# H3 convolution and linear attention on one core: the shift convolution of four chunks in two parts by time points, 11 of 16 on VectorE and 5 on POOL, and constants in ScalarE's instructions

## The chip, the core and the metric

One core of one Trainium2 chip runs the whole kernel in one launch. The metric is device microseconds from start to end of the program, the median of several runs. The core has five engines that work beside each other, each down a queue of its own: PE (TensorE, matrix products from SBUF into the eight banks of PSUM), DVE (VectorE) and POOL (GpSimd) for element-wise work, ACT (ScalarE) for element-wise functions, and SP (SyncE), which here only issues transfers. An instruction starts when those ahead of it on its engine are done and when the data it reads, and the place it writes to, have been given free by the others.

## The reference, cut

Two blocks that don't depend on each other, over S = 2048 time points and D = 576 channels; their results stand side by side in the output.

```python
def A(q, k, v, shift_k, ssm_k, ssm_D):                  # H3
    k_pad = pad(k, 3 zeros ahead in time)
    k_shift = sum over t of k_pad[:, t:t+S, :] * shift_k[:, 3-t]   # four taps for each channel
    kv = k_shift * v
    y = irfft(rfft(kv, 2S) * rfft(ssm_k, 2S))[:S]        # long convolution, as long as the sequence
    y = y + kv * ssm_D
    return q * y

def B(x, wqkv, wo):                                      # linear attention, 32 heads of 18
    q, k, v = x @ wqkv
    phi = lambda t: where(t > 0, t + 1, exp(t)) + 1e-6
    pq, pk = phi(q), phi(k)
    kv, z = sum over s of pk[s] v[s]^T, sum over s of pk[s]
    return ((pq @ kv) / (pq @ z + 1e-6)) @ wo

out = concat([A(...), B(...)], axis=-1)
```

## The kernel before, in words

**Layout.** Block A is cut into five chunks of channels (`ACH`: four of 128, one of 64). q, k and v lie in SBUF with 128 blocks of time on the partitions, and in each partition 16 time points by the channels. A chunk's k or v is thus 128 x 16 x 128, 2048 elements in a partition (1024 for the last chunk). k comes in two groups (`GRP`: 256 channels, chunks 0 and 1, then 320), which use one buffer in turn.

**The shift convolution** is the unit `cv.chunk.stage.engines`, function `conv`. Stage 0 multiplies k by tap 0 into `a_`. Stages 1 to 3 multiply the shifted k by their tap into `t_` and add `t_` to `a_`. Stage 3 then writes v = `a_` * v over v. That makes eight operations for a chunk, all `tensor_tensor` with both inputs in SBUF. Each letter of the code names the engine of one operation, D for VectorE and P for POOL. `a_` and `t_` are the two halves of the tile `at`, of which there is one buffer. In the profile the multiplications of stage 0 are L492, those of the other stages L494, the additions L495, and the product with v L498.

**The long convolution** is a transform in two steps for the filter h (codes with h) and for v (codes with u). `u1`/`h1` (function `s1`, L537) multiplies one time point at a time, `v[:, b, :]`, by the matrix G: eight matmuls for half of the time points. The result goes from PSUM to the tile `Cu` or `Ch`; `ut`/`ht` transposes it by a transfer; `u2`/`h2` (L560) is the second step, into `SU` or `T`. `pX`, `pT`, `pS`, `pA` (function `prod`: X L572, T L574, S and A L577) form the product of the two spectra, on VectorE or POOL, from SBUF to SBUF. `i1` (L594) and `i2` (L607, L608) go back, and `i2` ends with the product with q on VectorE (L609).

**Block B.** `k.r` (L456) and `q.g.half`, `qt` (L465, L473) project x, of which four transposed groups xT come in turn, two in SBUF at a time; the last step for a group is a memset of one row on POOL (L354). Each projection ends with `phi`: ScalarE takes the exponential from PSUM (L448), then VectorE takes min and max of that and the PSUM bank (L449). Only then is the bank free. `G` (L662) multiplies x by pk; it ends with a copy of one column on VectorE (L652), then a copy on ScalarE (L653). `hc` are constants for the heads, made on POOL (L85 to L102).

**Order.** Nothing is left to a scheduler. The list `ORDER` is written by hand, and its units are recorded one after the other; each engine then runs its own instructions in that order. The digits behind a slash in a unit are places: each names which PSUM slot (0 to 3, two banks each) or which tile of a ring the unit takes. TensorE's unit that takes a slot waits until the engine that last read it is done.

A projection's end, with the bank free behind the second line:

```python
nc.scalar.activation(out=out_ap, in_=ps_ap, func=ACT.Exp, bias=K.neg1[0:n, :])
nc.vector.scalar_tensor_tensor(out=out_ap, in0=out_ap, scalar=1.0, in1=ps_ap, op0=ALU.min, op1=ALU.max)
```

Of the kernel before, what the change touches and what calls it, by code (L numbers as in the profile page):

```python
# [31 lines left out]
ORDER = """  # L32
io ls ix.0.0/0 sin.1.0 wu.1.A/0 wu.2.B/1 dl ix.1.0/1 sin.0.0 hl.0/0 dc/2 hd.0 Wj.A/301 ix.0.1 id xl.2 iw ix.1.1 sin.0.1
hl.1/1 hT.0.D/22 xd.2.DA/030 hd.1 h1.0.0.0.A/11 h1.0.1.0.D/2 hT.1.D/00 wm iv sin.1.1 xl.0 h1.0.0.1.A/3 xd.0.DA/112
h1.0.1.1.A/0 wk lw.1 sw W lw.2 k.11/3 hl.2/1 hd.2 lw.0 k.9/2 k.2/0 k.1/1 k.10/3 kl.0 h1.1.1.1.A/02 k.8/0 cv.0.0.D es
cv.0.1.DD hc h1.1.1.0.A/1 h1.1.0.1.A/3 q.2.1/2 xl.3 q.0.1/0 k.0/1 h1.1.0.0.A/3 ht.0.0/0 qt.0/2 ht.0.1/1 h2.0.1.1.A/00
cv.0.2.PD vl.0/0 cv.0.3.DDD h2.0.1.0.A/3 eps ql.0/1 q.2.0/1 hl.3/2 xd.3.AA/020 q.0.0/3 k.3/2 ht.1.1/1 u1.0.1.1.A/10
k.15/1 u1.0.1.0.A/3 hT.2.D/00 u1.0.0.1.A/2 u1.0.0.0.A/1 cv.1.0.P cv.1.1.DD k.13/3 cv.1.2.DD h2.1.1.1.A/10 h2.1.1.0.A/2
q.3.1/1 h2.0.0.1.A/20 xd.1.T/1 h2.0.0.0.A/3 cv.1.3.DDP q.3.0/2 ut.0.0/1 u2.0.0.0.A/00 q.1.0/3 k.7/1 k.6/0 FT.0.T
u2.0.0.1.A/2 ut.0.1/0 pX.0.0.D/0 qt.1/3 u2.0.1.0.A/11 u2.0.1.1.D/0 k.12/2 u1.1.1.0.A/11 kl.1 k.5/3 u1.1.0.1.A/0  # L40
pX.0.1.D/1 k.14/1 ht.1.0/1 xl.1 u1.1.0.0.A/2 u1.1.1.1.A/3 cv.2.0.D hl.4/1 pT.0.1.D k.4/0 h1.2.1.0.A/02 pS.0.1.D ut.1.1/0
h1.2.1.1.A/1 cv.2.1.DD pT.0.0.P hd.3 pS.0.0.D q.1.1/3 h2.1.0.0.A/32 h2.1.0.1.A/0 G.1/1 cv.2.2.DP h1.2.0.0.A/2 pA.0.1.N
h1.2.0.1.A/0 u2.1.1.1.D/03 zs/01 ut.1.0/1 u2.1.1.0.A/2 pA.0.0.N i1.0.0.0.D/13 i1.0.0.1.A/0 i1.0.1.0.A/1 zz/2
i1.0.1.1.A/3 pX.1.1.D/0 pA.1.1.N vl.1/0 cv.2.3.DDD ht.2.0/0 pT.1.1.D u2.1.0.1.A/10 u2.1.0.0.A/2 ht.2.1/1 FT.1.T
hT.3.a/02 hd.4 G.3/1 cv.3.0.D cv.3.1.DD u1.2.0.0.A/03 lwv pS.1.1.D u1.2.1.1.A/0 G.0/2 cv.3.2.DD u1.2.1.0.A/1 pX.1.0.D/1
pA.1.0.N u1.2.0.1.A/3 G.4/0 h2.2.1.1.A/22 cv.3.3.DDD h2.2.1.0.A/1 ut.2.0/1 G.2/3 h2.2.0.0.D/00 wom lwo i2.0.1/2
h2.2.0.1.A/1 u2.2.0.0.A/03 i2.0.0/0 h1.3.0.1.D/11 ut.2.1/0 h1.3.0.0.A/2 h1.3.1.0.A/3 kv/0 u2.2.0.1.A/2 h1.3.1.1.A/1
pT.1.0.D pS.1.0.D i1.1.1.1.A/03 hT.4.p/01 i1.1.1.0.A/0 cv.4.0.D den/2 cv.4.1.PP ht.3.1/1 u2.2.1.1.D/11 i1.1.0.1.D/3
i1.1.0.0.A/0 pX.2.0.D/0 u2.2.1.0.A/1 M.2.A/2 i2.1.0/3 i2.1.1/0 M.3.A/1 ht.3.0/0 h2.3.1.1.A/12 bc.2/31 st.0 u1.3.1.1.A/00
# [176 lines left out]
def _sine(tc, cpool, K, ri, h):  # L226
    b = slice(8 * h, 8 * h + 8)
    if ri not in K.G:
        K.G[ri] = cpool.tile([128, 16, 128], BF, name="G%d" % ri)
# [1 line left out]
    tc.nc.scalar.activation(out=K.G[ri][:, b], in_=src, func=ACT.Sin, scale=TWO_PI / 8192, bias=K.negpi[:])  # L231
# [22 lines left out]
def kernel(  # L254
# [190 lines left out]

    def phi(ps_ap, out_ap, n):

        nc.scalar.activation(out=out_ap, in_=ps_ap, func=ACT.Exp, bias=K.neg1[0:n, :])  # L448
        nc.vector.scalar_tensor_tensor(out=out_ap, in0=out_ap, scalar=1.0, in1=ps_ap, op0=ALU.min, op1=ALU.max)  # L449

    def b_k(r):
        ps = psum.tile([128, 1024], FP32, name="k_ps")
        rr = r % 4
# [4 lines left out]
        phi(ps[:, 0:D], pk[:, r, 0:D], 128)

    def b_q(g, half):  # L460
        ps = psum.tile([128, 2, 512], FP32, name="q_ps")
        for j in range(2):
            c = 2 * half + j
            for t in range(5):
                nc.tensor.matmul(ps[:, j, :], lhsT=wqk[:, t, 128 * c:128 * c + 128], rhs=xT[g][:, t, :],  # L465
                                 start=(t == 0), stop=(t == 4))
        phi(ps[:], pqT[:, 2 * half:2 * half + 2, g * 512:(g + 1) * 512], 128)

    def b_qt(p):
        ps = psum.tile([128, 512], FP32, name="qt_ps")  # L470
        for t in range(5):
            for i, g in enumerate(PAIR[p]):
                nc.tensor.matmul(ps[64 * i:64 * i + 64, :], lhsT=wqk[:, t, 512:576], rhs=xT[g][:, t, :],  # L473
                                 start=(t == 0), stop=(t == 4))
        phi(ps[:], pq4[:, p, :], 128)


    def conv(ci, stage, eng='DDD'):
# [12 lines left out]
        if stage == 0:
            on[0].tensor_tensor(out=a_, in0=kk[:, 3:19], in1=wb(0), op=ALU.mult)  # L492
        else:
            on[0].tensor_tensor(out=t_, in0=kk[:, 3 - stage:19 - stage], in1=wb(stage), op=ALU.mult)  # L494
            on[1].tensor_tensor(out=a_, in0=a_, in1=t_, op=ALU.add)  # L495
# [399 lines left out]
```

## Time and profile before

| | |
|---|---|
| runs | 157.4, 157.73 and 157.91 us, median 157.73 |
| profiled execution | its span is 156.1 us; the runs' times take in about 1.6 us around the span |
| PE | 148.3 us busy, 95% of the span |
| DVE | 134.2 us, 86% |
| ACT | 130.8 us, 84% |
| POOL | 60.3 us, 39% |
| granted TensorE clock | full in every slice |

Busy time is work done, not work that sets the end: an engine can be busy with something that has time. The stage of the convolutions lies between 23 us, when k has landed, and 100 us. The chain of work that ended last has 62% of its time on PE, 12% on transfers, 11% on ScalarE, 8% on VectorE and 1% on POOL. Rows of a timeline give start, length, engine, line and instruction, the output behind the arrow's head and inputs behind its tail; grouped rows give count, then busy time and the mean in ns.

### The profile page before, as it was taken

Reading aid. Unit: us, or ns where it says so; the run is one execution under the profiler, and the core shown is the slowest. Engines: PE = TensorE matmul, PEld = TensorE weight load, DVE = VectorE, ACT = ScalarE, POOL = GpSimd, SP = SyncE. Lnnn points to the kernel's source line nnn. Section 1 sums busy time; section 2 is a strip of 40 time slices with the busy share of each in tenths; the row PEclk is TensorE's granted clock in tenths of the full one; section 3 lists DMA queues with packets and bytes.
Section 4 is the critical chain, followed back from the end, with each engine's and each line's share of the span. In section 5 each row is a group of like instructions: output and inputs, shape, how many; then the busy total and the mean of one; then the engine's idle time right before and its main releaser. Section 6 shows DMA issues by size and latency. Waiting matters only on the chain.

```text
span 156.1 us, 4608 instructions
## 1 busy us (share of the span) xinstructions
PE 148.3 (95%) x1986; PEld 90.6 (58%) x1986; DVE 134.2 (86%) x169; ACT 130.8 (84%) x162; POOL 60.3 (39%) x70
## 2 busy tenths in 40 slices
PE   7999999999999999999999999999988999999990
PEld 2686564466633456457566558767555656568650
DVE  6989769899899798997899999899999979997530
ACT  4999999989998899959999767997998978897431
POOL 6038701908310974007300019457999050230000
PEclk9999999999999999999999999999999999999999
DMA  2997999999999699999999879977779997636086
GB/s 92 380 294 188 296 300 145 252 296 281 201 178 234 135 312 235 166 231 302 178 171 199 220 134 232 144 139 136 231 156 179 149 325 187 156 117 182 0 231 197
DMA packets 74315, 31.92 MB, mean 204 GB/s; under 512 B 52090, under 2 KB 73653, under 8 KB 74294
## 3 DMA queue, kind: packets, MB, share of 16 engines
q1 hardware_dynamic: 74294, 31.62, 90.7%
q8 instruction: 15, 0.25, 0.6%
q14 instruction: 6, 0.05, 0.1%
HBM read 14.97 MB, written 4.72 MB: 126 GB/s over the span
## 4 chain that ended last, share of the span: by engine, by line
PE 62%; DMA 12%; ACT 11%; DVE 8%; issue 2%; POOLq 2%; POOL 1%; SPq 1%; DVEq 0%; ACTq 0%
PE k_ps L456 10%; PE g_ps L662 10%; PE s_ps L537 8%; PE q_ps L465 6%; DMA q<-in_A_q_dram 6%; PE i_ps L594 5%; PE s_ps L560 4%; PE o_ps L783 4%; DMA Cth<-Ch 3%; DMA Ctu<-Cu 3%; DVE q L609 2%; DVE pqT L753 2%; PE i_ps L607 2%; PE i_ps L608 2%; ACT G L231 2%
## 5 line engine op out<-in xcount | busy, mean ns | idle before, releaser
L456 PE MATMUL k_ps<-wqk,xT 128*128 128x512 bf16 (+1 forms) x160 | 21.5, 286 | 0.0
L537 PEld LDWEIGHTS <-G 128*128 128x128 bf16 x320 | 17.2, 98 | 3.1 <-issue 2.3
L465 PE MATMUL q_ps<-xT,wqk 128*128 128x512 bf16 x80 | 18.4, 380 | 0.0
L309 ACT ACTIVATE Cu<-s_ps 128x1024 bf16<-128x1024 f32 (+1 forms) x19 | 17.3, 957 | 0.4 <-PE s_ps L537 0.2
L456 PEld LDWEIGHTS <-xT 128*128 128x128 bf16 x160 | 11.4, 98 | 10.5 <-issue 0.3
L662 PE MATMUL g_ps<-pk,x_sb 128*128 128x512 bf16 (+1 forms) x128 | 16.5, 286 | 0.0
L309 ACT ACTIVATE V<-i_ps 128x1024 bf16<-128x1024 f32 x16 | 15.5, 1025 | 1.1 <-PE i_ps L594 0.8
L309 ACT ACTIVATE Ch<-s_ps 128x1024 bf16<-128x1024 f32 (+1 forms) x17 | 15.7, 952 | 0.3 <-PE s_ps L537 0.3
L309 ACT ACTIVATE T<-s_ps 128x1024 bf16<-128x1024 f32 x15 | 14.8, 1026 | 0.8 <-PE s_ps L560 0.7
L309 ACT ACTIVATE ob<-o_ps 128x576 bf16<-128x576 f32 (+1 forms) x14 | 8.8, 635 | 7.4 <-PE o_ps L775 4.2
L783 PE MATMUL o_ps<-wo_M,pqT 128*128 128x512 bf16 (+1 forms) x112 | 15.0, 287 | 0.0
L495 DVE TENSOR_TENSOR at<-at 128x2048 bf16<-128x2048 bf16 (+1 forms) x12 | 14.2, 1181 | 0.9 <-POOL at L494 0.4
L449 DVE SCALAR_TENSOR_TENSOR pk<-pk,k_ps 128x576 bf16<-128x576 bf16 x16 | 11.9, 752 | 3.4 <-ACT pk L448 3.2
L309 ACT ACTIVATE SU<-s_ps 128x1024 bf16<-128x1024 f32 x14 | 14.1, 1027 | 0.7 <-PE s_ps L560 0.6
L494 DVE TENSOR_TENSOR at<-k,Wj 128x2048 bf16<-128x2048 bf16 (+1 forms) x12 | 14.1, 1171 | 0.0
L495 POOL TENSOR_TENSOR at<-at 128x1024 bf16<-128x1024 bf16 (+1 forms) x3 | 8.3, 2772 | 14.0 <-DVE at L494 10.9
L609 DVE TENSOR_TENSOR q<-i_ps,q 128x1024 bf16<-128x1024 f32 (+1 forms) x10 | 11.0, 1114 | 3.1 <-PE i_ps L608 2.8
L662 PEld LDWEIGHTS <-x_sb 128*128 128x128 bf16 x128 | 8.4, 97 | 8.9 <-issue 1.2
L448 ACT ACTIVATE pk<-k_ps,neg 128x576 bf16<-128x576 f32 x16 | 11.6, 741 | 1.5 <-PE k_ps L456 1.0
L465 PEld LDWEIGHTS <-wqk 128*128 128x128 bf16 x80 | 7.4, 98 | 9.2 <-issue 1.5
L783 PEld LDWEIGHTS <-pqT 128*128 128x128 bf16 x112 | 7.5, 98 | 7.9 <-issue 1.2
L594 PE MATMUL i_ps<-W,T 64*128 64x128 bf16 x160 | 11.2, 217 | 0.6 <-DVE pqT L753 0.5
(163 smaller groups left out, 336.0 us busy)
## 6 DMA issues: line engine op xcount, KB each, us to landing
x_sb<-in_B_x_dram SPq DMA_DIRECT2D x4, 576.0 KB, 6.9
h_sb<-in_A_ssm_k_dram SPq DMA_DIRECT2D x4, 512.0 KB, 5.8
out_dram<-ob SPq DMA_DIRECT2D x7, 288.0 KB, 4.0
k<-in_A_k_dram SPq DMA_DIRECT2D x1, 1280.0 KB
v<-in_A_v_dram SPq DMA_DIRECT2D x1, 1280.0 KB
q<-in_A_q_dram SPq DMA_DIRECT2D x1, 1280.0 KB, 8.6
wqk<-in_B_wqkv_dram SPq DMA_DIRECT2D x2, 576.0 KB, 8.4
k<-in_A_k_dram SPq DMA_DIRECT2D x1, 1024.0 KB, 8.8
```

The source lines that it names most:

```text
L309: nc.scalar.activation(out=out, in_=in_, func=ACT.Copy)
L448: nc.scalar.activation(out=out_ap, in_=ps_ap, func=ACT.Exp, bias=K.neg1[0:n, :])
L449: nc.vector.scalar_tensor_tensor(out=out_ap, in0=out_ap, scalar=1.0, in1=ps_ap, op0=ALU.min, op1=ALU.max)
L456: nc.tensor.matmul(ps[:, n0:n1], lhsT=xT[r // 4][:, t, rr * 128:(rr + 1) * 128], rhs=wqk[:, t, D + n0:D + n1], start=(t == 0), stop=(t == 4))
L465: nc.tensor.matmul(ps[:, j, :], lhsT=wqk[:, t, 128 * c:128 * c + 128], rhs=xT[g][:, t, :], start=(t == 0), stop=(t == 4))
L494: on[0].tensor_tensor(out=t_, in0=kk[:, 3 - stage:19 - stage], in1=wb(stage), op=ALU.mult)
L495: on[1].tensor_tensor(out=a_, in0=a_, in1=t_, op=ALU.add)
L537: nc.tensor.matmul(ps[:, bi, 0:dc], lhsT=K.G[ri][:, b, :], rhs=xf(b), start=True, stop=True)
L594: nc.tensor.matmul(ps[:, r, g, :], lhsT=s[key, hf][64 * r:64 * r + 64, z, x, 128 * g:128 * g + 128], rhs=K.W[64 * r:64 * r + 64, m, :], st ...
L609: nc.vector.tensor_tensor(out=qs, in0=ps[:, :, 0:dc], in1=qs, op=ALU.mult)
L662: nc.tensor.matmul(ps[:, n0:n1], lhsT=x_sb[:, r, f0:f0 + fn], rhs=pk[:, r, n0:n1], start=(r == 0), stop=(r == 15))
L783: nc.tensor.matmul(pss[i][:, n0:n1], lhsT=pqT[:, c, r * 128:(r + 1) * 128], rhs=B['M'][:, c, n0:n1], start=(c == 0 and not first), stop=(c ...
```

## The change

Two things. Every operation of the convolution of chunks 0 to 3 (engine code `S`) is split over the 16 time points: points 0 to 10, 1408 elements in a partition, on VectorE, and points 11 to 15, 640 elements, on POOL. Chunk 4 keeps its codes. And two constants, -pi in the sines and -1 in the exponential of phi, are given in the ScalarE instruction and no longer as a tile of one column. No unit changes its place in `ORDER`; in the profile after, all operations of the convolution have one line, L487, and the lines behind it are three higher.

```diff
-cv.0.0.D ... cv.0.1.DD ... cv.0.2.PD ... cv.0.3.DDD          (the same codes in ORDER for chunks 1 to 3)
+cv.0.0.S ... cv.0.1.SS ... cv.0.2.SS ... cv.0.3.SSS
...
-    tc.nc.scalar.activation(out=K.G[ri][:, b], in_=src, func=ACT.Sin, scale=TWO_PI / 8192, bias=K.negpi[:])
+    tc.nc.scalar.activation(out=K.G[ri][:, b], in_=src, func=ACT.Sin, scale=TWO_PI / 8192, bias=-math.pi)
...
-    nc.scalar.activation(out=K.sm[:, 1536:1984], in_=K.wi, func=ACT.Sin, scale=TWO_PI / 16, bias=K.negpi[:])
+    nc.scalar.activation(out=K.sm[:, 1536:1984], in_=K.wi, func=ACT.Sin, scale=TWO_PI / 16, bias=-math.pi)
...
-        nc.scalar.activation(out=out_ap, in_=ps_ap, func=ACT.Exp, bias=K.neg1[0:n, :])
+        nc.scalar.activation(out=out_ap, in_=ps_ap, func=ACT.Exp, bias=-1.0)
...
-        on = [nc.gpsimd if e == 'P' else nc.vector for e in eng]
+        def on(n, o, i0, i1, op):
+            for p, b0, b1 in ((0, 0, 11), (1, 11, 16)) if eng[n] == 'S' else ((eng[n] == 'P', 0, 16),):
+                (nc.gpsimd if p else nc.vector).tensor_tensor(out=o[:, b0:b1], in0=i0[:, b0:b1], in1=i1[:, b0:b1], op=op)
...
-            on[0].tensor_tensor(out=a_, in0=kk[:, 3:19], in1=wb(0), op=ALU.mult)
+            on(0, a_, kk[:, 3:19], wb(0), ALU.mult)
...
-            on[0].tensor_tensor(out=t_, in0=kk[:, 3 - stage:19 - stage], in1=wb(stage), op=ALU.mult)
-            on[1].tensor_tensor(out=a_, in0=a_, in1=t_, op=ALU.add)
+            on(0, t_, kk[:, 3 - stage:19 - stage], wb(stage), ALU.mult)
+            on(1, a_, a_, t_, ALU.add)
...
-            on[2].tensor_tensor(out=u, in0=a_, in1=u, op=ALU.mult)
+            on(2, u, a_, u, ALU.mult)
```

VectorE's queue at chunk 0, a piece of the difference (rows with `at` are the convolution, `pk`, `pqT` and `pq` phi; two rows of one form that follow each other are told as x2):

```order
 L449 SCALAR_TENSOR_TENSOR pk<-pk,k_ps 128x576 x6
-L492 TENSOR_TENSOR at<-k,Wj 128x2048
-L494 TENSOR_TENSOR at<-k,Wj 128x2048
-L495 TENSOR_TENSOR at<-at 128x2048
+L487 TENSOR_TENSOR at<-k,Wj 128x1408 x2
+L487 TENSOR_TENSOR at<-at 128x1408
 L449 SCALAR_TENSOR_TENSOR pqT<-pqT,q_ps 128x2x512 x2
 L449 SCALAR_TENSOR_TENSOR pk<-pk,k_ps 128x576
 L449 SCALAR_TENSOR_TENSOR pq_77<-pq_77,qt_ps 128x512
-L495 TENSOR_TENSOR at<-at 128x2048
```

The convolution's places among VectorE's phi operations stay, with 1408 elements in place of 2048.

POOL's queue at chunk 0, a piece of the difference that begins with the last of the head constants and ends with the memset of an xT:

```order
 L101 MEMSET onesr 128x32
 L102 MEMSET onesr 128x8
-L494 TENSOR_TENSOR at<-k,Wj 128x2048
+L487 TENSOR_TENSOR at<-k,Wj 128x640
+L487 TENSOR_TENSOR at<-at 128x640
+L487 TENSOR_TENSOR at<-k,Wj 128x640
+L487 TENSOR_TENSOR at<-at 128x640
+L487 TENSOR_TENSOR v<-at,v 128x5x128
 L396 MEMSET pk 128x16
 L354 MEMSET xT 1x512
```

POOL had one whole operation of chunk 0 here and now has five parts, the last of which writes v; three more parts stand ahead of the head constants (before L85, where POOL had no convolution). The memset of xT comes behind all eight.

POOL's queue at chunk 2 before, from the memset of the second k buffer on (T is the product of chunk 0's spectra, `hp` the filter of chunk 4):

```order
L408 MEMSET k 1x960
L574 TENSOR_TENSOR T<-SU,T 128x2048
L495 TENSOR_TENSOR at<-at 128x2048
L644 MEMSET wo_M 128x576
L523 COPY hp<-h_sb 64x2048
```

And after:

```order
L408 MEMSET k 1x960
L487 TENSOR_TENSOR at<-k,Wj 128x640 x2
L487 TENSOR_TENSOR at<-at 128x640
L577 TENSOR_TENSOR T<-SU,T 128x2048
L487 TENSOR_TENSOR at<-k,Wj 128x640
L487 TENSOR_TENSOR at<-at 128x640
```

T was the first work behind the memset and now comes behind three parts of chunk 2's convolution, which wait for the second k.

More of the change, by code (lines that the diff above doesn't have):

```diff
@@ L34 @@
 hl.1/1 hT.0.D/22 xd.2.DA/030 hd.1 h1.0.0.0.A/11 h1.0.1.0.D/2 hT.1.D/00 wm iv sin.1.1 xl.0 h1.0.0.1.A/3 xd.0.DA/112
[L35 to L38, printed above, removed]
@@ L39 @@
-q.3.1/1 h2.0.0.1.A/20 xd.1.T/1 h2.0.0.0.A/3 cv.1.3.DDP q.3.0/2 ut.0.0/1 u2.0.0.0.A/00 q.1.0/3 k.7/1 k.6/0 FT.0.T
+h1.0.1.1.A/0 wk lw.1 sw W lw.2 k.11/3 hl.2/1 hd.2 lw.0 k.9/2 k.2/0 k.1/1 k.10/3 kl.0 h1.1.1.1.A/02 k.8/0 cv.0.0.S es
+cv.0.1.SS hc h1.1.1.0.A/1 h1.1.0.1.A/3 q.2.1/2 xl.3 q.0.1/0 k.0/1 h1.1.0.0.A/3 ht.0.0/0 qt.0/2 ht.0.1/1 h2.0.1.1.A/00
+cv.0.2.SS vl.0/0 cv.0.3.SSS h2.0.1.0.A/3 eps ql.0/1 q.2.0/1 hl.3/2 xd.3.AA/020 q.0.0/3 k.3/2 ht.1.1/1 u1.0.1.1.A/10
+k.15/1 u1.0.1.0.A/3 hT.2.D/00 u1.0.0.1.A/2 u1.0.0.0.A/1 cv.1.0.S cv.1.1.SS k.13/3 cv.1.2.SS h2.1.1.1.A/10 h2.1.1.0.A/2
@@ L40 @@
+q.3.1/1 h2.0.0.1.A/20 xd.1.T/1 h2.0.0.0.A/3 cv.1.3.SSS q.3.0/2 ut.0.0/1 u2.0.0.0.A/00 q.1.0/3 k.7/1 k.6/0 FT.0.T
 u2.0.0.1.A/2 ut.0.1/0 pX.0.0.D/0 qt.1/3 u2.0.1.0.A/11 u2.0.1.1.D/0 k.12/2 u1.1.1.0.A/11 kl.1 k.5/3 u1.1.0.1.A/0
-pX.0.1.D/1 k.14/1 ht.1.0/1 xl.1 u1.1.0.0.A/2 u1.1.1.1.A/3 cv.2.0.D hl.4/1 pT.0.1.D k.4/0 h1.2.1.0.A/02 pS.0.1.D ut.1.1/0
-h1.2.1.1.A/1 cv.2.1.DD pT.0.0.P hd.3 pS.0.0.D q.1.1/3 h2.1.0.0.A/32 h2.1.0.1.A/0 G.1/1 cv.2.2.DP h1.2.0.0.A/2 pA.0.1.N
+pX.0.1.D/1 k.14/1 ht.1.0/1 xl.1 u1.1.0.0.A/2 u1.1.1.1.A/3 cv.2.0.S hl.4/1 pT.0.1.D k.4/0 h1.2.1.0.A/02 pS.0.1.D ut.1.1/0
@@ L43 @@
+h1.2.1.1.A/1 cv.2.1.SS pT.0.0.P hd.3 pS.0.0.D q.1.1/3 h2.1.0.0.A/32 h2.1.0.1.A/0 G.1/1 cv.2.2.SS h1.2.0.0.A/2 pA.0.1.N
 h1.2.0.1.A/0 u2.1.1.1.D/03 zs/01 ut.1.0/1 u2.1.1.0.A/2 pA.0.0.N i1.0.0.0.D/13 i1.0.0.1.A/0 i1.0.1.0.A/1 zz/2
-i1.0.1.1.A/3 pX.1.1.D/0 pA.1.1.N vl.1/0 cv.2.3.DDD ht.2.0/0 pT.1.1.D u2.1.0.1.A/10 u2.1.0.0.A/2 ht.2.1/1 FT.1.T
-hT.3.a/02 hd.4 G.3/1 cv.3.0.D cv.3.1.DD u1.2.0.0.A/03 lwv pS.1.1.D u1.2.1.1.A/0 G.0/2 cv.3.2.DD u1.2.1.0.A/1 pX.1.0.D/1
-pA.1.0.N u1.2.0.1.A/3 G.4/0 h2.2.1.1.A/22 cv.3.3.DDD h2.2.1.0.A/1 ut.2.0/1 G.2/3 h2.2.0.0.D/00 wom lwo i2.0.1/2
+i1.0.1.1.A/3 pX.1.1.D/0 pA.1.1.N vl.1/0 cv.2.3.SSS ht.2.0/0 pT.1.1.D u2.1.0.1.A/10 u2.1.0.0.A/2 ht.2.1/1 FT.1.T
@@ L47 @@
+hT.3.a/02 hd.4 G.3/1 cv.3.0.S cv.3.1.SS u1.2.0.0.A/03 lwv pS.1.1.D u1.2.1.1.A/0 G.0/2 cv.3.2.SS u1.2.1.0.A/1 pX.1.0.D/1
+pA.1.0.N u1.2.0.1.A/3 G.4/0 h2.2.1.1.A/22 cv.3.3.SSS h2.2.1.0.A/1 ut.2.0/1 G.2/3 h2.2.0.0.D/00 wom lwo i2.0.1/2
 h2.2.0.1.A/1 u2.2.0.0.A/03 i2.0.0/0 h1.3.0.1.D/11 ut.2.1/0 h1.3.0.0.A/2 h1.3.1.0.A/3 kv/0 u2.2.0.1.A/2 h1.3.1.1.A/1
```

## The prediction

> **What bounds the kernel now.** I read the page's busy shares first, then a table of busy time by stage, then the rows of single instructions. The page's lines:
>
> ```profile
> span 156.1 us, 4608 instructions
> PE 148.3 (95%) x1986; PEld 90.6 (58%) x1986; DVE 134.2 (86%) x169; ACT 130.8 (84%) x162; POOL 60.3 (39%) x70
> ```
>
> A share over the span hides the stage in which the convolution runs, so next the stage table (window, length, then busy us and count of each engine, clock, DMA share, GB/s):
>
> ```profile
> 23.00:42.00 19.00, 18.71 (x177) 10.96 (x175) 17.69 (x17) 17.77 (x20) 8.74 (x4) 1.00 1.11 231
> 42.00:62.00 20.00, 19.60 (x198) 9.60 (x196) 18.26 (x19) 17.88 (x22) 9.47 (x4) 1.00 1.03 220
> 62.00:82.00 20.00, 20.00 (x315) 12.22 (x313) 18.49 (x22) 18.14 (x19) 4.07 (x1) 1.00 1.18 212
> 82.00:100.00 18.00, 18.00 (x272) 12.07 (x272) 16.94 (x27) 14.09 (x18) 6.56 (x3) 1.00 0.89 193
> ```
>
> From 23 to 100 us TensorE is busy 76.3 of 77 us, VectorE 71.4. So TensorE sets the end; at most 0.7 us can be gained there, and every time TensorE stands still in this stage is added to the end. VectorE is close behind: TensorE gets a PSUM bank back only when VectorE has read it.
>
> What a faster VectorE would do therefore matters less than how VectorE and POOL get on with each other. These rows of the timelines (start, length, engine, line, instruction) decide it:
>
> ```profile
> 56.35 4.07 POOL L574 TENSOR_TENSOR T<-SU,T 128x2048 bf16<-128x2048 bf16 x1 [1.10 <-DVE X L572]
> 59.90 1.59 DVE L572 TENSOR_TENSOR X<-SU,T 128x2048 bf16<-128x2048 bf16 x1
> 55.05 1.23 DVE L572 TENSOR_TENSOR X<-SU,T 128x2048 bf16<-128x2048 bf16 x1 [0.16 <-ACT SU L309]
> 135.27 0.68 DVE L577 TENSOR_TENSOR X<-X 128x1024 bf16<-128x1024 bf16 x1
> 135.50 2.44 POOL L577 TENSOR_TENSOR T<-T 128x1024 bf16<-128x1024 bf16 x1 [7.03 <-DVE T L574]
> 126.35 2.12 POOL L577 TENSOR_TENSOR X<-X 128x1024 bf16<-128x1024 bf16 x1 [5.57 <-DVE X L572]
> ```
>
> VectorE's X takes 1.23 us alone, but 1.59 where it starts under a POOL operation: POOL ends at 60.42, X at 61.49, 1.07 later, about the streaming time of the whole X. It had done nothing until POOL was through. The other way round, POOL's 2.12 became 2.44 behind VectorE's X, which ended at 135.95; POOL ended 1.99 after that. So two operations that both read two SBUF tensors exclude each other; I take that for all of them. Operations of VectorE that read PSUM run at their usual length beside POOL. Before, nearly every POOL operation lies beside such ones.
>
> [...]
>
> **The change, part by part.**
>
> ```profile
> L494 DVE TENSOR_TENSOR at<-k,Wj 128x2048 bf16<-128x2048 bf16 x11 | 13.4, 1216 | 0.0
> L494 DVE TENSOR_TENSOR at<-k,Wj 128x1024 bf16<-128x1024 bf16 x1 | 0.7, 680 | 0.0
> L494 POOL TENSOR_TENSOR at<-k,Wj 128x2048 bf16<-128x2048 bf16 x1 | 4.1, 4067 | 7.7 <-DVE at L495 7.7
> L494 POOL TENSOR_TENSOR at<-k,Wj 128x1024 bf16<-128x1024 bf16 x2 | 4.2, 2118 | 0.0
> ```
>
> (1) Prices, on the straight line through two sizes. VectorE's 1408 elements: 0.68 + 384 x 0.536/1024 = 0.88 us. POOL's 640: 2.12 - 384 x 1.949/1024 = 1.39 us. Under the exclusion the start-up lies under the other's work: VectorE holds 1408/2048 x 1.07 = 0.74, POOL 1.39 less the 0.13 that 2.12 lost = 1.25. One operation in two parts thus costs 1.99 us where both queues are in it, against 1.22 before. Unhidden, even the POOL part alone (1.39) is longer than the old whole operation. Ends: 1.33 (640/1024 of 2.12) and 1.6 for POOL; I take 1.39, since two rows give it.
>
> (2) Balance. VectorE had 28 of the 32 operations, 28 x 1.22 = 34 us, and now 32 x 0.88 = 28: 6 us less. POOL loses 4 x 4.07 and gets 32 x 1.39: 28 us more. Time in which the shared way is held: before 28 x 1.07 + eight products of chunks 0 and 1 on VectorE (some 8) + 5 x 4.07 = 58 us; after 32 x 0.74 + 8 + 32 x 1.25 + 4 = 76 us, for a stage that lasted from 23.0 to 92.8. So 6 us more at perfect packing, and no packing is perfect. That is the low end of the exclusion case.
>
> (3) Where TensorE waits. I walk VectorE's and POOL's queues down in their new order, by turns where both want the way.
>
> Chunk 0:
>
> ```profile
> 16.08 0.19 POOL L85 MEMSET maskbd<- 128x126 bf16 x1
> 19.09 0.10 POOL L102 MEMSET onesr<- 128x8 bf16 x1
> 23.01 1.23 DVE L492 TENSOR_TENSOR at<-k,Wj 128x2048 bf16<-128x2048 bf16 x1 [0.45 <-DMA k<-in_A_k_dram]
> 26.55 2.34 DVE L449 SCALAR_TENSOR_TENSOR pqT<-pqT,q_ps 128x1024 bf16<-128x1024 bf16 x2
> 28.81 0.75 DVE L449 SCALAR_TENSOR_TENSOR pk<-pk,k_ps 128x576 bf16<-128x576 bf16 x1
> 36.60 0.61 PE L537 MATMUL s_ps<-v,G 128*128 128x128 bf16 x8
> ```
>
> k lands at 23.0. Three pairs end on VectorE at 27.8, on POOL at 29.0. VectorE's phi operations (1.13 apart, 0.7 for the short ones) take it to 31.4. POOL does its head constants, which ran from 16.08 to 19.19 before and now stand behind the first three parts: to 32.1. Then five pairs by turns: 31.4 + 5 x 1.99, POOL's v part ends at 41.4. TensorE's s1 of that v starts at 36.60; its fourth matmul (time point 11) is at 36.77: **+4.7**. The memset of an xT, behind it in POOL's queue, and VectorE's late phi hold the next unit back equally, so no order of the two avoids it.
>
> Chunk 1:
>
> ```profile
> 43.61 0.75 DVE L449 SCALAR_TENSOR_TENSOR pk<-pk,k_ps 128x576 bf16<-128x576 bf16 x1
> 44.99 0.62 PE L560 MATMUL s_ps<-Cth,W 64*32 64x512 bf16 x16
> 53.25 0.41 PE L560 MATMUL s_ps<-Ctu,W 64*32 64x512 bf16 x8
> 53.59 1.27 PE L473 MATMUL qt_ps<-xT,wqk 128*64 128x512 bf16 x10
> ```
>
> VectorE reaches it at 46.4, goes by turns with POOL, and ends the pk of 43.61 at 51.8; the bank is wanted by the second half of 44.99, at 45.27 + 4.7: **+1.8**. Two banks more (53.25 and 53.59) come back at 60.0 and 61.2: **+1.1**. Delay so far 7.6.
>
> Chunk 2: the product T, 4.07 on POOL, ran at 56.35, before the chunk's k was touched. Now it is behind three conv parts:
>
> ```profile
> 64.36 0.74 DVE L449 SCALAR_TENSOR_TENSOR pk<-pk,k_ps 128x576 bf16<-128x576 bf16 x1
> 65.19 0.62 PE L560 MATMUL s_ps<-Cth,W 64*32 64x512 bf16 x16
> 68.61 1.21 DVE L449 SCALAR_TENSOR_TENSOR pqT<-pqT,q_ps 128x1024 bf16<-128x1024 bf16 x1
> 70.69 0.41 PE L560 MATMUL s_ps<-Ctu,W 64*32 64x512 bf16 x8
> 72.48 0.23 PE L594 MATMUL i_ps<-W,T 64*128 64x128 bf16 x2
> ```
>
> T holds the way from 71.3 to 75.3; VectorE's own T goes after it and the pk of 64.36 ends at 77.0, wanted at 65.47 + 7.6: **+4.0**. Three more turns, and the pqT of 68.61 ends at 85.0, wanted at 70.69 + 11.6: **+2.8**. The copies that follow it free the banks of 71.03 and 72.48 late: **+1.1**.
>
> Chunk 3: VectorE's small copies, on which the G banks hang, stand among eight turns:
>
> ```profile
> 88.15 0.62 PE L560 MATMUL s_ps<-Cth,W 64*32 64x512 bf16 x16
> 92.76 0.41 PE L560 MATMUL s_ps<-Cth,W 64*32 64x512 bf16 x8
> 94.33 0.40 PE L560 MATMUL s_ps<-Ctu,W 64*32 64x512 bf16 x8
> ```
>
> These find their banks free 0.8, 1.6 and 2.3 us later each than the delay that they inherit: **+4.7**. Behind them the order is as before and I carry the delay to the end. Sum of the four: 4.7 + 2.9 + 7.9 + 4.7 = 20.2.
>
> With POOL's part at 1.33 or 1.6 instead of 1.39 the same walk gives some 18 and 28.
>
> (4) Constants in the instruction:
>
> ```profile
> L448 ACT ACTIVATE pqT<-q_ps,neg 128x1024 bf16<-128x1024 f32 x8 | 8.9, 1115 | 1.8 <-PE q_ps L465 1.7
> L309 ACT ACTIVATE T<-s_ps 128x1024 bf16<-128x1024 f32 x15 | 14.8, 1026 | 0.8 <-PE s_ps L560 0.7
> 9.38 0.34 PE L537 MATMUL s_ps<-hT,G 128*128 128x128 bf16 x3 [0.38 <-ACT G L231]
> ```
>
> Same size, with and without a bias tile: 0.09 us each. 26 exponentials and 5 sines make 2.8 us of ScalarE, which waits for TensorE anyway and so gives nothing, but for the sines: three stand in a row ahead of the matmul at 9.38, which waits for the last: -0.3. (Ends: 0, -0.4.)
>
> Sum: 156.1 - 0.3 + 20.2 = 176.0. The runs' median, 157.7, is 1.6 above the span: **177.6**.
>
> **Rivals.**
>
> No exclusion of the short parts: then both chains run freely, and POOL's is 23.0 + 8 x 1.39 + 3.1 + some 0.3 = 37.4 at the matmul of 36.77. +0.8 there, 0.3 later: 158.5. For it: only two overlaps of length show the exclusion. Against: both fit to 0.1 us.
>
> The way is shared in turns finer than an instruction, or one queue packs better than by turns: between the 6 of (2) and 15: 164 to 172.
>
> Faster: without exclusion, and with POOL's 640 at 1.30 or less (1.33 is its lower end), POOL's v is there in time, TensorE never waits, and what is left is the head's 0.3 and part of the 0.7: 157. It decides at 36.77; the four-microsecond rows speak against it.
>
> Half clock: TensorE's stalls of 4.7 and 4.0 us could slow it.
>
> ```profile
> 1.06 3.60 PE L79 MATMUL warm_ps<-sm 128*128 128x512 bf16 x9 [1.06 <-DVE negpi L129]
> 45.54 2.33 PE L465 MATMUL q_ps<-xT,wqk 128*128 128x512 bf16 x10
> ```
>
> The nine warm-up matmuls stand 0.43 us apart, ten of the same size later 0.22: after standing still TensorE went at half rate for some 3.5 us, though the clock column says 1.00. Two or three such stalls cost 1.75 us each: 181 to 183. [...]
>
> **Chances.** Exclusion by turns without half clock 0.50, with it 0.25, better packing 0.13, no exclusion 0.08 (a quarter of that within 0.3%), faster 0.02, no difference 0.02. What a measurement here can tell from no change is about 0.3%, 0.5 us. Faster 0.02, same 0.04, slower 0.94. The range takes the packing bound and the dearer POOL part: 165 to 188.
>
> **What would show it.** Lines L487 in the profile after: VectorE's mean far above 0.88 (near 1.7 to 2), POOL's above 1.39; TensorE waiting for POOL at the s1 of chunk 0 near 41 us and its idle time in the four stages near 5, 3, 8 and 5 us; POOL's T ending after 75 us; exponentials 0.09 shorter. If L487 shows 0.88 and 1.39 instead, the exclusion is wrong and with it the forecast.

## The result, and the profile after

The changed kernel takes 187.88 us (median of 4 runs, 187.19 to 189.82) against 157.82 for the kernel before. The ratio is 1.192, interval 1.186 to 1.198. The forecast was 177.6 with a range up to 188: the direction and the exclusion by turns were right, the size was 10 us too small. The profiled execution has a span of 186.6 us, 30.5 more than before. (In some executions the half rate of the first matmuls lasts longer, in the trace of chunk 3 alone to 13.0 us with 7 or 8 matmuls in a half-microsecond where the changed kernel has some 12, and the convolution is reached later, by 1.9 us in the trace of the fillers in chunk 0, so that the medians of the kernel before lie between 157.8 and 159.2 from one group of runs to the next; the ratios are to the runs before on the same chip, and leave out executions more than 1.5% above the fastest of their kernel.)

The page after: the span, the busy shares, and the row of the granted clock in 40 slices.

```profile
span 186.6 us, 4625 instructions
PE 157.7 (85%) x1968; PEld 97.7 (52%) x1986; DVE 159.0 (85%) x173; ACT 129.0 (69%) x162; POOL 103.7 (56%) x98
PEclk9999999975999999995599987957999999999999
```

VectorE has fewer elements to do in the convolution, and it is busy 24.8 us more (134.2 before). TensorE is busy 9.4 us more with the same matmuls, and its clock, full throughout before, falls in four places. The stage of the convolution, in the columns of the table before:

```profile
23.00:42.00 19.00, 14.18 (x116) 7.78 (x116) 18.13 (x15) 12.68 (x14) 18.02 (x23) 0.93 1.18 240
42.00:62.00 20.00, 17.20 (x148) 9.24 (x148) 15.90 (x14) 13.60 (x15) 13.47 (x10) 0.90 0.56 111
62.00:82.00 20.00, 17.71 (x199) 10.41 (x199) 19.22 (x16) 14.10 (x18) 13.60 (x6) 1.00 1.03 204
82.00:100.00 18.00, 12.73 (x200) 8.31 (x201) 14.90 (x15) 10.81 (x11) 7.43 (x5) 0.72 0.63 101
```

TensorE stood still for 0.7 of these 77 us before and does so for 15.2 now. The parts, grouped by form (count, busy us, mean ns, idle before):

```profile
L487 POOL TENSOR_TENSOR at<-k,Wj 128x640 bf16<-128x640 bf16 x16 | 29.2, 1835 | 25.7 <-DMA k<-in_A_k_dram 14.9 <-DVE v L487 10.3
L487 DVE TENSOR_TENSOR at<-k,Wj 128x1408 bf16<-128x1408 bf16 x16 | 25.0, 1575 | 0.0
L487 DVE TENSOR_TENSOR at<-at 128x1408 bf16<-128x1408 bf16 x12 | 18.2, 1520 | 0.4
```

VectorE's 1408 elements take longer than the 2048 did (1.22). Single rows show how, first where the two queues meet, then where each is alone:

```profile
33.90 1.92 POOL L487 TENSOR_TENSOR at<-at 128x640 bf16<-128x640 bf16 x1
35.90 1.92 POOL L487 TENSOR_TENSOR at<-k,Wj 128x640 bf16<-128x640 bf16 x1
34.60 1.96 DVE L487 TENSOR_TENSOR at<-at 128x1408 bf16<-128x1408 bf16 x1
31.67 0.89 DVE L487 TENSOR_TENSOR at<-at 128x1408 bf16<-128x1408 bf16 x1
46.09 1.40 POOL L487 TENSOR_TENSOR at<-k,Wj 128x640 bf16<-128x640 bf16 x1
```

Alone they take 0.89 and 1.40. Together each takes 1.92 to 1.97, and POOL's starts stand 2.00 apart, with one operation of VectorE in each such stretch: they go by turns, each waiting for the whole of the other. TensorE's five longest waits (in brackets the idle time and what ended it):

```profile
38.62 0.34 PE L540 MATMUL s_ps<-v,G 128*128 128x128 bf16 x3 [1.80 <-DVE v L487]
41.35 0.69 PE L540 MATMUL s_ps<-v,G 128*128 128x128 bf16 x5 [2.38 <-POOL v L487]
54.44 0.41 PE L563 MATMUL s_ps<-Cth,W 64*32 64x512 bf16 x8 [2.48 <-DVE pk L449]
86.51 0.63 PE L563 MATMUL s_ps<-Ctu,W 64*32 64x512 bf16 x8 [5.37 <-DVE pqT L449]
122.35 0.63 PE L563 MATMUL s_ps<-Ctu,W 64*32 64x512 bf16 x8 [4.42 <-ACT wv_GT L656]
```

Where the 30.5 us lie: the two traces cut at the same matmuls, and each stretch split into the time in which TensorE's rows leave a gap and the time in which they don't (us, after less before).

| from (before) | to | longer by | of it waiting | of it slower matmuls | the walk had |
|---|---|---|---|---|---|
| 0 | 26.0, head | -0.2 | -0.2 | 0.0 | -0.3 |
| 26.0 | 37.1, chunk 0's s1 | 4.9 | 4.5 | 0.4 | 4.7 |
| 37.1 | 65.2, chunk 1 | 4.5 | 2.8 | 1.7 | 2.9 |
| 65.2 | 85.1, chunk 2 | 10.5 | 7.3 | 3.2 | 7.9 |
| 85.1 | 100.0, chunk 3 | 10.9 | 6.3 | 4.7 | 4.7 |
| 100.0 | 152.5, the rest | -0.1 | 0.5 | -0.6 | 0 |

The trace after lacks the records of some twenty matmuls, each of which leaves a gap of at most 0.2 us, so the split of a stretch is good to a few tenths.

### The profile page after: what moved, and what is told of

The parts are those of the page before. It is cut to its first block, busy times and chain, and to the rows that moved or that the text cites. A ratio compares the mean times of both kernels' runs of the same rounds, so it can differ in the third digit from the quotient of the medians.

```text
span 186.6 us, 4625 instructions
## 1 busy us (share of the span) xinstructions
PE 157.7 (85%) x1968; PEld 97.7 (52%) x1986; DVE 159.0 (85%) x173; ACT 129.0 (69%) x162; POOL 103.7 (56%) x98
## 4 chain that ended last, share of the span: by engine, by line
PE 40%; DVE 34%; POOL 10%; issue 6%; DMA 5%; ACT 2%; SPq 1%; POOLq 0%; DVEq 0%
DVE at L487 15%; PE o_ps L786 7%; POOL at L487 7%; PE i_ps L597 7%; DMA k<-in_A_k_dram 5%; PE s_ps L540 5%; DVE pqT L756 4%; DVE T L580 4%; PE k_ps L456 3%; PE s_ps L563 3%; DVE pqT L449 2%; PE i_ps L610 2%; PE warm_ps L79 2%; PE g_ps L665 2%; PE hT_ps L519 2%
## 5 line engine op out<-in xcount | busy, mean ns | idle before, releaser
L487 POOL TENSOR_TENSOR at<-k,Wj 128x640 bf16<-128x640 bf16 (+1 forms) x18 | 33.4, 1867 | 26.6 <-DMA k<-in_A_k_dram 14.9
L487 POOL TENSOR_TENSOR at<-at 128x640 bf16<-128x640 bf16 (+1 forms) x14 | 25.9, 1848 | 10.3 <-DVE at L487 9.3
L487 DVE TENSOR_TENSOR at<-k,Wj 128x1408 bf16<-128x1408 bf16 (+1 forms) x18 | 26.3, 1476 | 0.0
L487 DVE TENSOR_TENSOR at<-at 128x1408 bf16<-128x1408 bf16 (+1 forms) x13 | 18.9, 1456 | 0.4
L665 PE MATMUL g_ps<-pk,x_sb 128*128 128x65 bf16 (+1 forms) x124 | 17.9, 300 | 0.7 <-ACT Cu L309 0.5
L656 ACT ACTIVATE wv_GT<-g_ps,ex 128x576 bf16<-128x576 f32 x5 | 3.7, 740 | 20.9 <-DVE ex L655 20.9
L563 PE MATMUL s_ps<-Ctu,W 64*32 64x512 bf16 x144 | 7.3, 419 | 9.8 <-DVE pqT L449 5.4
L540 PE MATMUL s_ps<-v,G 128*128 128x128 bf16 (+1 forms) x160 | 11.2, 221 | 4.4 <-POOL v L487 2.4
L786 PE MATMUL o_ps<-wo_M,pqT 128*128 128x64 bf16 (+1 forms) x106 | 14.1, 281 | 0.6 <-issue 0.5
L563 PEld LDWEIGHTS <-W 64*32 64x32 bf16 x288 | 4.0, 89 | 19.6 <-issue 18.1
```

Of the source, the lines that this page charges most:

```text
L487: (nc.gpsimd if p else nc.vector).tensor_tensor(out=o[:, b0:b1], in0=i0[:, b0:b1], in1=i1[:, b0:b1], op=op)
L540: nc.tensor.matmul(ps[:, bi, 0:dc], lhsT=K.G[ri][:, b, :], rhs=xf(b), start=True, stop=True)
L563: nc.tensor.matmul(ps[q:q + 32, z, :], lhsT=K.W0[64 * z:64 * z + 64, x, :], rhs=Ct[64 * z:64 * z + 64, r, :, j, :], start=True, stop=True)
L665: nc.tensor.matmul(ps[:, n0:n1], lhsT=x_sb[:, r, f0:f0 + fn], rhs=pk[:, r, n0:n1], start=(r == 0), stop=(r == 15))
L786: nc.tensor.matmul(pss[i][:, n0:n1], lhsT=pqT[:, c, r * 128:(r + 1) * 128], rhs=B['M'][:, c, n0:n1], start=(c == 0 and not first), stop=(c ...
```

## The experiments

**Is it the constants?** The kernel before with the two constants alone (-math.pi in the sines likewise):

```diff
-... func=ACT.Exp, bias=K.neg1[0:n, :])
+... func=ACT.Exp, bias=-1.0)
```

> The kernel before with the constants alone in ScalarE's instructions, no split. My theory: 0.09 us less for each of 31 ScalarE instructions, all of it hidden except at the sines of the head: 0.2 to 0.3 us less, 157.4 to 157.6 us, which is hardly to be told from no change. Rival: part of the slowdown is from the constants: then over 158.5.

157.98 us over 12 runs against 158.82; ratio 0.995, interval 0.989 to 1.000. The constants cost nothing. A gain of some tenths is neither excluded nor shown.

**Is it the cut, or POOL?** Both parts on VectorE:

```diff
-            for p, b0, b1 in ((0, 0, 11), (1, 11, 16)) if eng[n] == 'S' ...
+            for p, b0, b1 in ((0, 0, 11), (0, 11, 16)) if eng[n] == 'S' ...
```

> The changed kernel with both parts of each operation on VectorE (11 and 5 points, two instructions each), POOL's part gone from POOL. Exclusion between VectorE and POOL as the cause: parts at about 0.88 and 0.45 us, nothing stretched; VectorE has some 9 us more work than before in a stage with 5.6 us free, so 160 to 164 us, clock at 1.00. Rival, that the cut into two instructions with its dependences is the cause: 180 to 188.

161.82 us, ratio 1.018 (1.006 to 1.030), as expected. The same parts, all on one engine:

```profile
L487 DVE TENSOR_TENSOR at<-k,Wj 128x1408 bf16<-128x1408 bf16 x16 | 14.1, 881 | 0.0
L487 DVE TENSOR_TENSOR at<-k,Wj 128x640 bf16<-128x640 bf16 x16 | 7.7, 481 | 0.0
```

0.88 instead of 1.58. The cut with its dependences is not the cause; POOL beside VectorE is. A control, the kernel with the constants alone and each operation whole and on VectorE:

```diff
-cv.0.2.PD ... cv.1.0.P ... cv.1.3.DDP ... cv.2.2.DP
+cv.0.2.DD ... cv.1.0.D ... cv.1.3.DDD ... cv.2.2.DD
```

> Neither split nor shared: every operation of chunks 0 to 3 whole on VectorE, the constants in the instructions. VectorE has four operations more than before, 4.9 us, against 9 us more in the kernel that cuts each in two: 158.5 to 160.5 us if VectorE's load is what counts, under 157.5 if POOL's four operations before were themselves a burden by the exclusion.

163.18 us (160.95 to 163.89), ratio 1.018 (1.003 to 1.032): every run is above what I expected, and it is no better than the cut kernel. Against the kernel before, both traces lose the same 3 us at the same three places, in chunks 0, 1 and 2, where VectorE does what POOL did before. So the four whole operations on POOL, beside VectorE's work on PSUM, were worth about 3 us.

**Do the parts wait for each other's data, or for a shared way?** The convolution of chunks 0 to 3 is whole and on VectorE, and POOL gets other work after each stage, whose results nothing uses. In chunks 1 to 3 a small copy of VectorE's first product starts that work, and VectorE's next addition waits for the copy; chunk 0 has no such tie:

```diff
+    def aside(ci, stage, kk, d0):
...
+        if ci and stage == 0:
+            nc.gpsimd.tensor_copy(out=side[:, 0:1, :], in_=st[ci]['at'][:, 0, 0:1, 0:64])
+        for i in range(2 * (1 if stage == 0 else 3 if stage == 3 else 2)):
+            if ci == 2:
+                for _ in range(6):
+                    nc.gpsimd.memset(side[:], 0.0)
+            elif ci == 1:
+                nc.gpsimd.tensor_copy(out=side[:], in_=kk[:, 14:19, 0:64])
+            else:
+                nc.gpsimd.tensor_tensor(out=side[:], in0=kk[:, 14:19, 0:64], in1=w, op=ALU.mult)
...
+        if ci == 3:
+            nc.vector.tensor_single_scalar(out=t_ if stage else a_, in_=kk[:, 3 - stage:19 - stage], scalar=0.5, op=ALU.mult)
```

> A probe of what excludes what. The convolution of chunks 0 to 3 is whole and on VectorE alone; POOL does other work beside it that no one reads (320 elements an instruction): in chunk 0 products of two tensors in SBUF, in chunk 1 copies of one, in chunk 2 memsets, in chunk 3 products of two again, while VectorE's multiplications there are by the number 0.5 (one input; the taps are left out in that chunk). As the prediction had it (both sides with two inputs): VectorE's 1.22 us becomes 1.7 to 2.0 in chunk 0 and stays 1.22 in chunk 1 and 2; chunk 3's one-input operations keep one length throughout. Theory after the changed kernel's trace, where a product on VectorE took 4.4 us beside a POOL copy: chunk 1 stretched as well, to 1.7 or more. Rival, that the parts wait for each other's data and not for a shared way: 1.22 in all chunks, since nothing here is shared. The whole time says little (POOL's queue is full of the added work): 165 to 195 us.

VectorE's operations, in this order: beside products on POOL (chunk 0), after them, when POOL has only its short head constants, beside copies (chunk 1), beside memsets (chunk 2), and with one input beside products (chunk 3):

```profile
25.71 1.70 DVE L513 TENSOR_TENSOR at<-at 128x2048 bf16<-128x2048 bf16 x1
32.48 1.23 DVE L513 TENSOR_TENSOR at<-at 128x2048 bf16<-128x2048 bf16 x1
57.24 1.36 DVE L513 TENSOR_TENSOR at<-at 128x2048 bf16<-128x2048 bf16 x1
84.56 1.23 DVE L513 TENSOR_TENSOR at<-at 128x2048 bf16<-128x2048 bf16 x1
130.13 1.20 DVE L507 TENSOR_SCALAR at<-k 128x2048 bf16<-128x2048 bf16 x1
```

The whole time is 211.5 us (one execution), above what I expected; VectorE waits 10.3 us in one piece for the small copy of chunk 3, which stands in POOL's queue behind chunk 2's memsets. POOL's added work writes nothing that VectorE reads, and the turns are there all the same (VectorE's 1.70 beside products, 1.23 after them), so it is a shared way and not the data. POOL's product of 320 elements takes 0.79 where VectorE reads PSUM and 1.65 in turns. POOL's copy of 320 takes 0.45 where VectorE reads PSUM and 1.33 in turns: a copy with one input takes the way too. VectorE is stretched less than I expected there (1.36, not 1.7), because that copy is short. Memsets leave VectorE at 1.23. Of VectorE's operations with one input, two beside memsets took 1.55 together, and beside products one alone takes 1.20. What I had used in the prediction, both sides with two inputs, is thus too narrow.

**What made chunk 3 dearer than the walk?** VectorE's product with v, and POOL beside it, in the changed kernel:

```profile
117.02 4.43 DVE L487 TENSOR_TENSOR v<-at,v 128x1408 bf16<-128x1408 bf16 x1
116.83 3.87 POOL L526 COPY hp<-h_sb 64x2048 bf16<-64x2048 bf16 x1
```

The copy of chunk 4's filter reads one tensor, and I had left it out. Behind that product in VectorE's queue stands the small copy that ScalarE waits for, and on ScalarE hangs the bank of TensorE's wait of 4.42. First chunk 3 alone in two parts, chunks 0 to 2 as before:

```diff
-cv.3.0.D cv.3.1.DD cv.3.2.DD cv.3.3.DDD
+cv.3.0.S cv.3.1.SS cv.3.2.SS cv.3.3.SSS
```

> Chunk 3 alone in two parts, chunks 0 to 2 as before, constants in the instructions. In the changed kernel this chunk cost TensorE 6.3 us of waiting and 4.6 of slower matmuls, where my walk had 4.7 in all. If that is the chunk's own price (POOL's copy of a filter beside it, which I had left out, and the half clock): 165 to 169 us. If the delays of the chunks before have made it dearer: 161 to 163 us, near the walk.

169.39 us, ratio 1.066 (1.055 to 1.076), a little over the range of the first theory. The stretch from 85.1 to 100.0 is 10.5 us longer than before, 10.9 in the changed kernel: the price is the chunk's own. It is made up differently, though: 8.8 us of waiting and 1.8 of slower matmuls here, 6.3 and 4.7 there. Now the copy is kept away, by one unit of ORDER:

```diff
-hT.3.a/02 hd.4 G.3/1 ... hT.4.p/01
+hT.3.a/02 G.3/1 ... hd.4 hT.4.p/01
```

> The changed kernel with one ScalarE instruction of chunk 4's filter (the addition of D to its first column) moved behind chunk 3's convolution in the list, so that POOL's copy of that filter (3.87 us) can't start beside VectorE's last operations of chunk 3. If that copy holds VectorE's product with v: that product takes 0.9 us and not 4.43, TensorE's wait of 4.42 us falls to about 1, and with it goes the half clock behind it (2.7 us): 181 to 184 us. Rival, that the product waits for POOL's part of the convolution or for data: 187 to 189 us, the product still 4 us long.

```profile
116.60 0.89 DVE L487 TENSOR_TENSOR v<-at,v 128x1408 bf16<-128x1408 bf16 x1
118.38 0.41 PE L563 MATMUL s_ps<-Ctu,W 64*32 64x512 bf16 x8 [1.55 <-ACT wv_GT L656]
136.63 0.52 PE L563 MATMUL s_ps<-Cth,W 64*32 64x512 bf16 x8 [4.89 <-DMA Cth<-Ch]
```

185.92 us, ratio 1.179 (1.169 to 1.190), 1.9 above the forecast, and by the intervals not told apart from the changed kernel. At the place itself it went as expected: the product takes 0.89, the wait is 1.55, the clock stays full behind it, and the stretch from 85.1 to 100.0 is 4.9 us longer than before instead of 10.9. Then 4.9 us go to a new wait. The copy now ends at 130.2, its transposition stands in SP's queue ahead of the two that TensorE needs next, and these start at 131.6.

**Does the price follow the size?** 14 and 2 points:

```diff
-((0, 0, 11), (1, 11, 16))
+((0, 0, 14), (1, 14, 16))
```

> The changed kernel with 14 of 16 time points on VectorE and 2 on POOL. By turns: an operation holds the way 0.94 us for VectorE and some 0.53 for POOL (the line through POOL's two sizes at 256 elements, less its start), 1.47 against 1.99: 17 us less held in 32 operations, and about as much less waiting, with fewer falls of the clock: 164 to 172 us. Rival, a fixed price for each hand-over between the two queues, whatever the size: 180 to 188 us.

168.02 us, ratio 1.064 (1.054 to 1.074), in the middle of the range by turns; the fixed price is out. In chunk 0 two waits of 0.4 and 0.5 us are left. The largest is 3.25 us in chunk 2, where one VectorE part takes 4.91 us behind POOL's whole T of 4.05.

**One chunk, and the clock.** Chunk 0 alone in two parts, chunks 1 to 3 as before:

```diff
-cv.0.0.D ... cv.0.1.DD ... cv.0.2.PD ... cv.0.3.DDD
+cv.0.0.S ... cv.0.1.SS ... cv.0.2.SS ... cv.0.3.SSS
```

> Chunk 0 alone in two parts, chunks 1 to 3 as before, constants in the instructions. My walk: 4.7 us of waiting at chunk 0's first step of v, and up to 2 us of half clock behind it: 162 to 164.5 us. Rival, that a single chunk's delay is made up further on because VectorE and POOL get ahead while TensorE stands still: under 161 us.

163.74 us, ratio 1.038 (1.031 to 1.046), as walked. From 45 us on every stretch is as long as before to 0.1 us or less, but for one that is 0.4 shorter: next to nothing is made up. Now fillers in that wait, matmuls of 512 columns into a bank that is free there:

```diff
+    def filler(n):
+        ps = psum.tile([128, 1024], FP32, name="fill_ps")
+        for _ in range(n):
+            nc.tensor.matmul(ps[:, 0:512], lhsT=K.G[0][:, 0, :], rhs=K.G[0][:, 0:4, :], start=True, stop=True)
...
-u1.0.1.1.A/10
+fl.20/0 u1.0.1.1.A/10
```

> Chunk 0 alone in two parts, with 20 matmuls that no one reads in TensorE's wait. Behind it all is as before, where TensorE sets the end, so what is saved must stay. If standing still halves the clock and that is paid in the end: the clock stays at 1.00, the delay behind the wait falls from 6.0 to 4.5 us, 1.1 to 1.6 us less than without fillers: 162.1 to 162.6 us. Rival, that a slow TensorE only uses up time which it would wait anyway: 163.3 to 163.9 us.

163.85 us, ratio 1.031 (1.022 to 1.040), the rival's range in time, and not told apart from the kernel without fillers. The traces show what the whole times don't. Without fillers, then with them (window, busy us of the engines, clock):

```profile
44.00:48.00 4.00, 4.00 (x51) 3.37 (x50) 2.17 (x3) 2.65 (x4) 1.66 (x2) 0.83 0.02 4
44.00:48.00 4.00, 4.00 (x53) 3.16 (x52) 2.82 (x4) 3.48 (x5) 2.28 (x2) 1.00 0.02 4
```

The stretch behind the wait (37.1 to 45.0 before) is 1.4 us longer than before without fillers and 0.15 shorter with them, 1.5 us. The kernel without fillers makes nothing up later; the one with them loses 0.6 at a gap before 83 us whose cause its trace doesn't name. And the profiled execution with fillers reached 26 us of the program 1.9 us later. The saving is shown in the trace and not in the time.

In the changed kernel I tried all three long waits, first like this:

```diff
+fl.20/0 u1.0.1.1.A/10 ... fl.22/2 u2.1.1.1.D/03 ... fl.18/1 h2.2.0.1.A/1
```

> The changed kernel with 60 matmuls more that no one reads, put into TensorE's three long waits (20 before chunk 0's first step of v, 22 before the second step at 86.5 us, 18 before the one at 122.4), in PSUM banks that are free there. If standing still is what halves the clock, the granted clock stays at 1.00 there and the 2.1, 3.3 and 2.7 us of slower matmuls behind those waits go: 179 to 182 us, the waits' ends unmoved. Rival, that the clock falls for another reason, or that the stall and not the clock is all of the loss: 187 to 190 us.

191.77 us, ratio 1.208 (1.198 to 1.217): the second group found its bank free only at 87.18 and ran to 92.0, itself in the way by 4.9 us. Moved forward:

```diff
+fl.20/0 u1.0.1.1.A/10 ... fl.20/2 h1.2.0.0.A/2 ... fl.18/1 h2.2.0.1.A/1
```

> The fillers again, with the second group moved: 20 matmuls before chunk 0's first step of v, 20 before the steps of h that stand ahead of the wait at 81 to 86.5 us, in a bank that is free by then, 18 before the last. In the first filler kernel the second group found its bank free only at 87.2 us and stood 4.9 us in the way itself. If the half clock is paid in the end: clock at 1.00 in those places and 181 to 184 us (2.1, 3.3 and 2.7 us less, some of it given back). Rival, that VectorE and POOL in turns bound these stages, and a slow TensorE only uses up time that it would wait anyway: 185.5 to 188.5 us with the clock at 1.00.

188.73 us, ratio 1.197 (1.188 to 1.205), 0.2 above the rival's range. It looks like the rival's case and isn't quite. Chunk 0 and chunk 3 did save, 1.1 and 2.5 us, though only 0.5 of the 1.1 is left where chunk 2's waits begin. But VectorE came earlier to chunk 2 and drew the worse turn:

```profile
72.34 5.07 DVE L577 TENSOR_TENSOR T<-SU,T 128x2048 bf16<-128x2048 bf16 x1
71.63 4.69 POOL L577 TENSOR_TENSOR T<-SU,T 128x2048 bf16<-128x2048 bf16 x1
```

In the changed kernel VectorE's T was in ahead of POOL's and took 2.42. Here it waits for the whole of it, TensorE stands 3.89 us at 78 and falls to half clock there; 2.8 more are lost late, at a transposition at 148. So the last group alone:

```diff
+fl.18/1 h2.2.0.1.A/1
```

> The changed kernel with the last group of fillers alone (18 matmuls in the wait that ends at 122.4 us), so that the turns of VectorE and POOL ahead of it stay as they were. If the half clock is paid: 2.5 us less at 127 us, 185.2 to 186 us. Rival, that transfers or VectorE bound the stage behind and take it back: 187 to 188.5 us.

184.49 us (183.24 to 185.60), ratio 1.163 (1.148 to 1.177), below the changed kernel's interval and below the range that I gave. The stretch behind the wait is 2.5 us shorter, as expected, and keeps that to the end. Another 2.4 us of this profiled execution lie ahead of the fillers, where its clock was at half for 10 us and the changed kernel's for 20.

No version beats the kernel before: the constants alone are the nearest, and not told apart from it.

## Why the prediction was right, and where it failed

**Right.** That the operations exclude each other, whole by whole; the prices (1.99 us for an operation in two parts, measured 2.00 from start to start; 0.88 and 1.39 alone, measured 0.89 and 1.40); that every wait of TensorE is added to the end; chunks 0 to 2 (15.5 us of waiting forecast, 14.6 measured); the end of POOL's v part (41.4, measured 41.30). The last owes something to luck: in the traces of the late copy, of chunk 0 alone and of the last group of fillers alone POOL drew the first turn of chunk 0, VectorE's part of v ended last, and TensorE waited 3.2 us for that. The rival without exclusion is out by the parts on one engine and by the work set beside it. The constants take 0.09 us off each exponential (1.115 to 1.025) and 0.2 off the head, nothing that the times can tell.

**Right in sum only.** In chunk 2 I had 4.0 us at the pk that stands behind T, and 2.8 and 1.1 later. Measured were 1.0 at that place and 5.4 at the pqT, since VectorE's T got its turn ahead of POOL's. Which queue draws first decides several microseconds (VectorE's T took 2.42 here, and 5.07 with the fillers moved forward) and can't be read from the order of the instructions.

**Failed: the half clock as a rival.** The sum of 177.6 had nothing for slower matmuls. The half clock stood beside it with a chance of 0.25, against 0.50 for none, and a price of 1.75 us for each of two or three stalls, 3.5 to 5.3. No row of the kernel before shows that a stall of 4.7 or 4.0 us halves the clock, or what that costs; it was my estimate from the start of the program, where matmuls of 512 columns stand 0.43 us apart. The half clock came, in four places and eight windows, for 6.83, 10.24, 3.42 and 6.83 us, and the matmuls took 9.4 us more. Not all of that was paid. In chunk 3, 1.9 us of it lie ahead of the last wait, and there they were free: from 104.74, where this stretch begins, to the end of that wait it is 17.6 us in the changed kernel and 17.7 in two kernels whose clock stayed full ahead of the wait (fillers in all three waits as first placed, and the last group alone). VectorE, in turns with POOL, works through this piece without a pause and sets its end. Behind the wait 2.5 us were paid. With 2.1 behind chunk 0's waits and 3.2 in chunk 2, the half clock can account for at most some 8 of the 10 us by which the forecast was low. I had also written that the clock column reads 1.00 at half rate; behind the stalls it reads 0.50. At the start it reads 1.00 because the trace of the kernel before has no record of the clock ahead of 4.10 us, and until there the matmuls show half rate, 3.0 us (0.43 us from start to start, and 0.26 between the last two of the nine).

**Failed: "both read two SBUF tensors".** The rule that I drew from two overlaps left out POOL's copy of the filter. Chunk 3's waiting was 6.3 us and not 4.7, and the last wait alone 4.42 for 2.3 forecast; with the copy out of the way it was 1.55. The 6.3 hide a part, since TensorE's slower matmuls ahead of the last wait used up time that it would have waited. With the clock full behind that wait, chunk 3's stretch is 8.4 to 8.5 us longer than before (the three kernels that fill it); with the copy away it is 4.9 in the one execution traced, and the walk had 4.7. The copy thus cost some 3.6 us of its own, and brought on the wait behind which the 2.5 us of half clock were paid.

What stays open: how much of the half clock of chunks 0 and 2 the whole time would lose. For chunk 0 a saving is shown in the trace but not in the time. In chunk 2 fillers change the turns; the kernel with the last group alone, whose execution had two half-rate windows there and not three, was 1.3 us shorter behind that wait and kept it.

## What to carry to other kernels

Before work is shared between VectorE and POOL, look in the trace for two of their SBUF operations side by side: if one ends a whole operation's length after the other, the two run one after the other and the share gains nothing (here 2.00 us for the two parts, 1.22 for the whole on VectorE), and POOL's best places are those where VectorE reads PSUM (0.79 us there for the product of 320 elements, 1.65 in turns). Count every POOL instruction that reads SBUF, copies of one tensor too (1.33 us in turns, 0.45 where VectorE reads PSUM). When a change makes TensorE wait as long as here (behind 1.80 and 2.38 us one after the other, behind 5.37 and behind 4.42 us the clock was at half, behind 2.48 us it was not), put slower matmuls behind the wait into the likeliest sum, not among the rivals, unless another engine sets the end of the piece that follows.

## What the runs showed of the hardware

The clock falls and rises on a fixed grid. Half-microsecond windows of the changed kernel (busy us, clock third from the end):

```profile
39.00:39.50 0.50, 0.00 (x0) 0.00 (x0) 0.50 (x1) 0.00 (x0) 0.50 (x1) 0.81 0.28 11
46.00:46.50 0.50, 0.50 (x10) 0.50 (x9) 0.00 (x0) 0.35 (x1) 0.42 (x2) 0.86 0.00 0
110.50:111.00 0.50, 0.45 (x2) 0.24 (x3) 0.50 (x1) 0.00 (x0) 0.48 (x1) 0.99 0.11 33
114.00:114.50 0.50, 0.50 (x2) 0.15 (x1) 0.50 (x3) 0.33 (x1) 0.50 (x1) 0.59 0.24 49
```

From such rows the edges are at 39.31, 46.14, 83.69, 93.93, 110.99, 114.41, 121.23 and 128.06 us. Less the first and divided by 3.413 (the 88.75 us from first to last, in 26 steps) that is 0, 2, 13, 16, 21, 22, 24 and 26, whole numbers to 0.01, and so in the traces of the fillers and of the late copy. The grid lies elsewhere in each execution. So it isn't one long gap that counts, but how little was done in a window. A gap of 2.48 us at 52 to 54.4, cut in two by the grid (an edge at 53.0), did nothing; three gaps of 0.8, 0.5 and 0.5 us between short runs of matmuls in one window (107.6 to 111.0) halved the clock. In all fourteen traces together, as long as matmuls were still to come, each of the 20 full-rate windows in which TensorE stood still for 1.77 us or more was followed by half rate (1.84, 2.15, 2.55 and 3.31 us in the changed kernel). Of those with less, none up to 1.52 us was; between 1.53 and 1.65 two were and six were not. The same waits can thus halve the clock in one execution and not in the next: the three gaps of chunk 3 did so here and with the fillers moved forward, and did not with the fillers as first placed, with the last group alone or with the late copy, where an edge of the grid cut them.
